# An attention stage and its first value products: order by priorities replaced by an order computed in the kernel from step durations

## The chip, the cores and the metric

The kernel runs on one core of one Trainium2 chip. The metric is the device time of one execution in microseconds (us), shown as the median of the runs. TensorE (PE, with its weight loads as PEld), VectorE (DVE), ScalarE (ACT) and GpSimd (POOL) compute; nearly all transfers are issued from the queue of SyncE (SP).

## What is computed

Everything is float32. Attention comes first, then two gated feed-forward layers on its result:

```python
B, H, S, D = (4, 8, 576, 64)
scores = where(causal, -1e9, q @ k.T / sqrt(D)); a = softmax(scores)
local  = a @ v
q_p    = where(q > 0, q, exp(q) - 1) + 1
mem    = (q_p @ M_prev) / (q_p . z_prev + 1e-6)
x      = sigmoid(beta) * mem + (1 - sigmoid(beta)) * local     # 2304 tokens x 512
x      = (sigmoid(x @ w_gate) * (x @ w_val)) @ w_out           # layer 1, 1536 wide
out    = (silu(x @ w_gate2) * (x @ w_val2)) @ w_out2           # layer 2
```

In most products both operands are held as a high part and a low part, and a product is the sum of three matmuls (high by high, high by low, low by high: `PASSES`). "Value products" are x @ w_val of layer 1; gate products are x @ w_gate.

## The kernel before, in words

**Attention.** The 8 heads of a batch make 4 pairs, two heads side by side on the partitions. A batch is worked in two kinds of units: 2 "head" units, each with the first 256 tokens of two pairs, and 4 "rest" units, each with the last 320 tokens of one pair (in the code, `Unit`, kinds `head` and `rest`; with `SPLIT = 4` all four batches are cut so). There are 24 units. A unit loads its q, k and v (`load`, line 143); turns q and k onto the partitions with TensorE and splits them into high and low parts (`turn`, lines 245 to 259; `turn_tail`, lines 261 to 275, for the last 64 tokens); makes the feature map e of q and scales it by its norm (`prep_e`, `prep_w`, lines 197 to 222), turning it in `turn_e` (lines 224 to 243); makes the scores of a block of 128 tokens and their softmax (`scores`, lines 285 to 338: products at 302 and 316, the running minimum on DVE at 303 and 319, the exponential on ACT at 325 and 330, two small DVE operations on the sums at 333 and 334, the scaling at 338 on POOL or DVE); turns the weights of the softmax (`probs`, lines 340 to 376, products at 355, 363, 370, 374); and sums the memory product and the values (`values`, lines 378 to 406, products at 387 and 396), from where the result goes to the DRAM buffer `xs` (line 408). Copies out of PSUM pass the helper `copy` (line 31 is its ACT branch, 35 and 37 its DVE and free ones), so they have those lines in the trace. PSUM has 8 banks: 3 for scores (`sc`), 3 for turned blocks (`tp`), 1 for `av`, 1 for the value products (`gv`).

The matmuls of line 316 use one half of TensorE's rows each (64 rows, two heads at once); those of line 396 one half of its columns; all others the whole array, but for the 64-token tails.

**Other work in the same stretch.** 24 weight blocks of layer 1 (12 of w_val, 12 of w_gate, each 128 x 512) come as 64-bit numbers and are turned to float32 on ACT and DVE (`Weights.turn`, lines 493 to 511: ACT at 500, four DVE operations at 503, 504, 507 and 511), and stored to the DRAM buffer `ws` (line 562); the w_val blocks are also split into high and low (line 603). The value products of the first 1152 tokens, in four pieces of 256, 320, 256 and 320 tokens, are made as soon as their tokens lie in `xs` (`Moe.load`, line 708; `Moe.values`, line 738, products at 749), each piece in 12 groups of 12 matmuls, each group emptied by ACT into `vo` and stored to the DRAM buffer `vs` (line 758).

**What sets the order.** `Attention.emit` (line 410) gives each step of each unit a due time from the tables `WHEN`, `WHEN0` and `SPAN` (in units of one unit's length) and writes the program in that order; the weight blocks and the four pieces join with due times from `EXTRA` (`Moe.extras`, line 760), the pieces 1 to 3 at 100 or later, and the w_gate loads are held back behind the loads of given units (`Weights.keep`, `gate_weight`). A scheduler of the framework then takes this program order as priorities and sets the real order on every engine, filling gaps with later work by its own estimate of durations. Which engine does a copy or a split is fixed in `ENGINE`, but for a few marked `any`.

**After it**, `Moe.run` (line 1043) makes the last 384 tokens' value products, prepares operands, and runs the two layers (lines 844, 995, 998); its order is pinned by `pinned` (line 953), which chains all instructions of each engine in program order.

Of the kernel before, what the change touches and what calls it, by code (L numbers as in the profile page):

```python
# [1 line left out]
WHEN = {'qk': -2.918, 'zm': -2.8, 'v': -0.622, 'pe': -1.766, 'pw': -1.489, 'pm': -1.092, 't0': -0.87, 't1': -0.45, 'te': 0.857, 's3': 0.004, 's2': 0.265, 's4': 0.5, 's1': 0.704, 's0': 0.85, 'p3': 0.476, 'p2': 0.809, 'p4': 0.938, 'p1': 0.919, 'p0': 1.1, 'v0': 1.112, 'v1': 1.339, 'store': 1.26, ('rest', 'v0'): 1.425, ('rest', 's4'): 0.378, ('head', 'v'): -1.263, ('rest', 'p1'): 0.628, ('rest', 's1'): -0.002, ('head', 'v0'): 1.122, ('rest', 'store'): 2.346, ('head', 's2'): 0.45, ('rest', 's0'): 0.08, ('head', 's4'): 0.733, ('rest', 'v1'): 1.114, ('rest', 'zm'): -2.421, ('rest', 'te'): 0.827, ('rest', 'pw'): -1.506}  # L2
WHEN0 = {'pm': -1.252, 'pe': -1.0, 'pw': -0.99, 'zm': -2.0, 't0': -1.2, 's0': 0.834, 'te': 0.682}
SPAN = {'head': (0.8, 0.85), 'rest': (0.734, 0.75), 'full': (0.866, 1.0)}
MZ = 1
BUFS = {'a_sm': 5, 'a_s': 6, 'a_xo': 1, 'a_pht': 1, 'a_ps': 3, 'a_pst': 3, 'w_raw': 2, 'w_cv': 2, 'm_vo': 2, 'm_gv': 1, 'm_x': 1, 'b_h': 4, 'b_hl': 3}
REUSE = dict(reuse_waits="tile")
SPLIT = 4
LATE = 4
EXTRA = {'gate': 0, 'rate': 0.3, 'w': 7.88, 'dw': 0.128, 'x0': 14.25, 'v0': 7.89, 'x1': 15.52}  # L10
# [32 lines left out]

NOSYNC = mybir.DependencyInfo(mybir.DependencyClass.NoSync, mybir.DependencyReason.DATA)


class Attention:
# [3 lines left out]
    def __init__(self, ctx, banks, tc, q, k, v, M_prev, z_prev, beta, xs):  # L51
# [48 lines left out]
        for r in range(2):  # L100
            t = cst.tile([128, 2, 128], F32R, name=f"qd{r}")
            nc.gpsimd.memset(t.bitcast(F32), 0.0)
            self.qd.append(t)
        g = self.g = cst.tile([128, H], F32, name="g")
# [28 lines left out]
        for p in range(0, self.NP, self.HP):  # L133
            if p < SPLIT * self.HP:
                self.units += [Unit("head", (p + i, p + i + 1)) for i in range(0, self.HP, 2)]
            self.units += [Unit("rest" if p < SPLIT * self.HP else "full", (p + i,)) for i in range(self.HP)]
        for n, u in enumerate(self.units):
            u.n = n
            u.lo, u.hi = dict(head=(0, 4), rest=(2, self.C), full=(0, self.C))[u.kind]
            u.b, u.hp = divmod(u.pairs[0], self.HP)  # L140
        self.st, self.loaded = {}, {}

    def load(self, u, names):
        nc = self.nc
        F, T = self.FULL, self.TAIL
        for n in names:
# [14 lines left out]
            if u.kind == "head":  # L161
# [7 lines left out]
                for c in range(2):  # L169
                    last = nc.sync.dma_start(  # L170
                        out=t[:, 2 * c:2 * c + 2].rearrange("p g h d -> p (g h) d"),
                        in_=src[2 * u.hp:2 * u.hp + 4, 128 * c:128 * c + 128].rearrange("h p d -> p h d"))
            else:
# [6 lines left out]
                last = nc.sync.dma_start(out=t[0:T, F], in_=s[:, 128 * F:].rearrange("h p d -> p h d"))  # L180
            setattr(u, n, t)
            if n == "q":
                self.loaded[u.n] = last.ins

    def prep_m(self, u):
        if u.kind == "rest":
            return
        for p in u.pairs:
            st = self.st.setdefault(p, {})
            mh = st["mh"] = self.mm.tile([128, 128], F32R, tag="mh", name="mh")  # L190
            ml = st["ml"] = self.mm.tile([128, 128], F32R, tag="ml", name="ml")
            m = u.m[:, p % self.HP]
            self.copy("mh", mh, m)
            self.two("ml", u).tensor_sub(ml, m, mh.bitcast(F32))

    def prep_e(self, u):

        nc = self.nc
        c = slice(u.lo, u.hi)
        q = u.q[:, c]  # L200
        u.e = self.ph.tile([128, self.C, 2, self.D], F32, tag="e", name="e")
        e = u.e[:, c]
        nc.vector.tensor_scalar(e, q, 0.0, None, op0=ALU.min)
        nc.scalar.activation(out=e, in_=e, func=ACTF.Exp)
        nc.vector.scalar_tensor_tensor(out=e, in0=q, scalar=0.0, in1=e, op0=ALU.max, op1=ALU.add)

    def prep_w(self, u):
        nc = self.nc
        n, g = u.hi - u.lo, len(u.pairs)
# [3 lines left out]
        e = by(u.e[:, u.lo:u.hi])  # L213
        w = by(self.ph.tile([128, self.C, 2, self.D], F32, tag="w", name="w")[:, 0:n])
        self.two("w", u).tensor_mul(w, e, u.z[:, hs].unsqueeze(1).to_broadcast(shp))
        f = self.sm.tile([128, 2 * self.C], F32, tag="f", name="f")[:, 0:2 * n]
        f = f.rearrange("p (c h) -> p c h", h=2 * g)
        nc.vector.tensor_reduce(out=f, in_=w, axis=mybir.AxisListType.X, op=ALU.add)
        nc.vector.tensor_scalar(f, f, 1e-6, None, op0=ALU.add)
        nc.vector.reciprocal(f, f)  # L220
        nc.vector.tensor_mul(f, f, self.g[:, hs].unsqueeze(1).to_broadcast(shp[:3]))
        nc.vector.tensor_mul(e, e, f.unsqueeze(3).to_broadcast(shp))

    def turn_e(self, u):
        nc = self.nc
        F, T, e = self.FULL, self.TAIL, u.e
        pt = u.pt = self.pht.tile([128, 2, self.S], F32R, tag="pt", name="pt")

        parts = dict(
            head=[[(2 * c + g, 256 * g + 128 * c) for g in range(2) for c in range(2)]],  # L230
            rest=[[(c, 128 * c) for c in range(2, F + 1)]],
            full=[[(c, 128 * c) for c in range(F)], [(F, 128 * F)]],
        )[u.kind]
        for part in parts:
            bank = self.pst.tile([128, 512], F32, tag="tp", name="tp")
            q0, n = part[0][1], 0
            for c, at in part:
                rows = T if c == F else 128
                n += rows
                nc.tensor.transpose(bank[:, at - q0:at - q0 + rows], e[0:rows, c].rearrange("p h d -> p (h d)"),  # L240
                                    self.idf[0:rows, 0:rows])
            self.copy("e", pt[:, 0, q0:q0 + n], bank[:, 0:n])
            nc.vector.tensor_sub(pt[:, 1, q0:q0 + n], bank[:, 0:n], pt[:, 0, q0:q0 + n].bitcast(F32))

    def turn(self, u, g):
# [3 lines left out]
        hp = u.pairs[g] % self.HP  # L249
        bank = self.pst.tile([128, 512], F32, tag="tp", name="tp")  # L250
        for i, t in enumerate((u.q, u.k)):
            for j, c in enumerate(cs):
                at = 128 * (n * i + j)
                self.nc.tensor.transpose(bank[:, at:at + 128], t[:, c].rearrange("p h d -> p (h d)"), self.idf)  # L254
        src = bank[:, 0:256 * n].rearrange("p (k t) -> p k t", k=2)
        to = slice(128 * c0, 128 * (c0 + n))
        hi, lo = (self.qka[:, hp, i, :, to] for i in range(2))
        self.copy("th", hi, src)
# [26 lines left out]
    def scores(self, u, g, i):  # L285
# [41 lines left out]
        else:  # L327
# [4 lines left out]
            r = sm  # L332
# [1006 lines left out]
```

## Time and profile before

| | us |
|---|---|
| median of three runs | 1140.15 (1139.62 to 1140.35) |
| the profiled execution, its time | 1140.23 |
| its span from first to last instruction | 1138.4 |
| attention stage, to the last store of attention | 0 to 362.5 |
| last value products and first operands | 362.5 to 394.5 |
| the two layers | 394.5 to 1138.4 |

The profiled execution is 0.08 us above the median; 1.83 us of its time lie outside the span. In the profile a busy PE is not a PE at its peak: ends of matmuls are modelled and overlap the next ones. In the chain of waits, matmuls that follow each other without a wait are spaced as they were really issued, so a piece of the chain gives the cost of a run of matmuls.

### The profile page before, as it was taken

Reading aid. Unit: us, or ns where it says so; the run is one execution under the profiler, and the core shown is the slowest. Engines: PE = TensorE matmul, PEld = TensorE weight load, DVE = VectorE, ACT = ScalarE, POOL = GpSimd, SP = SyncE. Lnnn points to the kernel's source line nnn. Section 1 sums busy time; section 2 is a strip of 40 time slices with the busy share of each in tenths; the row PEclk is TensorE's granted clock in tenths of the full one; section 3 lists DMA queues with packets and bytes.
Section 4 is the critical chain, followed back from the end, with each engine's and each line's share of the span. In section 5 each row is a group of like instructions: output and inputs, shape, how many; then the busy total and the mean of one; then the engine's idle time right before and its main releaser. Section 6 shows DMA issues by size and latency. Waiting matters only on the chain.

```text
span 1138.4 us, 19089 instructions
## 1 busy us (share of the span) xinstructions
PE 1097.5 (96%) x6416; PEld 995.3 (87%) x6416; DVE 806.4 (71%) x2020; ACT 599.7 (53%) x1472; POOL 167.8 (15%) x209
## 2 busy tenths in 40 slices
PE   7888999899999999999999999999999999999998
PEld 5666877777877899999999999999999999988886
DVE  7799867877966887887765654687877877653332
ACT  5657676566676765555543434555445445332222
POOL 3486543434233000000000000000000000000000
PEclk9689999999999999999999999999999999999999
DMA  5466436535722657666774333334443443654443
GB/s 132 143 180 198 137 90 191 155 119 152 216 57 72 230 153 262 221 218 221 241 256 135 94 95 105 120 94 139 139 149 120 157 132 117 214 172 124 124 124 105
DMA packets 162355, 173.77 MB, mean 153 GB/s; under 512 B 69328, under 2 KB 127696, under 8 KB 162256
## 3 DMA queue, kind: packets, MB, share of 16 engines
q1 hardware_dynamic: 162112, 172.54, 49.4%
q8 instruction: 51, 0.84, 0.3%
q14 instruction: 48, 0.39, 0.1%
q10 hardware_dynamic: 144, 0.00, 0.0%
HBM read 112.20 MB, written 60.29 MB: 152 GB/s over the span
## 4 chain that ended last, share of the span: by engine, by line
PE 77%; DMA 5%; DVE 4%; ACT 3%; issue 1%; SPq 1%; POOLq 0%; POOL 0%; ACTq 0%; DVEq 0%
PE ps L844 37%; PE ps L995 13%; PE ps L998 11%; PE gv L749 5%; PE sc L316 3%; PE av L396 3%; DMA raw<-in_moe_w_gate_dram 2%; PE tp L363 1%; DMA xraw<-xs 1%; PE av L387 1%; PE sc L302 1%; DMA raw<-ws 1%; PE tp L355 1%; PE tp L254 1%; PE tp L240 1%
## 5 line engine op out<-in xcount | busy, mean ns | idle before, releaser
L844 PE MATMUL ps<-xop,wset 128*128 128x384 f32 x2520 | 443.1, 336 | 6.6 <-ACT c L892 6.6
L844 PEld LDWEIGHTS ps<-xop,wset 128*128 128x128 f32 x2520 | 439.8, 188 | 8.9 <-ACT c L892 8.8
L981 DVE TENSOR_TENSOR hl<-hd,hl 128x384 fp32r<-128x384 f32 x144 | 80.3, 558 | 144.3 <-ACT hl L980 143.4
L980 ACT CAST hl<-hd 128x384 fp32r<-128x384 f32 x144 | 74.0, 514 | 179.8 <-PE ps L995 89.4
L892 ACT COPY c<-ps 128x384 f32<-128x384 f32 x180 | 86.2, 479 | 117.0 <-PE ps L844 115.7
L895 DVE TENSOR_TENSOR c<-ps,c 128x384 f32<-128x384 f32 x180 | 99.6, 554 | 43.3 <-ACT c L892 22.1
L749 PE MATMUL gv<-x,w 128*128 128x256 f32 (+2 forms) x720 | 127.1, 322 | 0.3
L749 PEld LDWEIGHTS gv<-x,w 128*128 128x128 f32 x720 | 109.8, 198 | 8.4 <-issue 4.2
L998 PE MATMUL ps<-hl,xop 128*128 128x384 f32 x648 | 114.0, 336 | 0.0
L998 PEld LDWEIGHTS ps<-hl,xop 128*128 128x128 f32 x648 | 112.6, 188 | 0.0
L995 PE MATMUL ps<-xop,hl 128*128 128x512 f32 x486 | 111.2, 389 | 0.0
L995 PEld LDWEIGHTS ps<-xop,hl 128*128 128x128 f32 x486 | 91.2, 188 | 19.0
L338 POOL TENSOR_SCALAR s<-s,sum,omg 128x512 f32<-128x512 f32 (+2 forms) x92 | 76.3, 840 | 105.0 <-DVE sum L334 50.7
L855 ACT ACTIVATE h<-c 128x384 f32<-128x384 f32 x108 | 56.7, 525 | 56.4 <-DVE c L895 53.0
L330 ACT ACTIVATE s<-s,nm 128x256 f32<-128x256 f32 (+3 forms) x128 | 71.8, 563 | 18.6 <-DVE nm L319 18.0
L316 PE MATMUL sc<-qka 64*128 64x128 f32 (+3 forms) x384 | 73.1, 372 | 8.3 <-DVE nm L319 7.4
L319 DVE CUSTOM_DVE_ANT_0 s<-sc,mask 128x256 f32<-128x256 f32 (+3 forms) x128 | 59.6, 484 | 14.8 <-PE tp L355 8.2
L316 PEld LDWEIGHTS sc<-qka 64*128 64x128 f32 x384 | 48.2, 201 | 24.1 <-DVE nm L319 9.2
L500 ACT ACTIVATE a<-raw 128x512 f32<-128x512 f32 x72 | 48.4, 672 | 31.9 <-DMA raw<-in_moe_w_gate_dram 19.2
L31 ACT COPY p<-tp 128x512 f32<-128x512 f32 x96 | 45.3, 496 | 18.1 <-PE av L396 7.7
L507 DVE SCALAR_TENSOR_TENSOR a<-raw,a 128x512 int32<-128x512 int32 x72 | 51.5, 715 | 0.2
L511 DVE SCALAR_TENSOR_TENSOR a<-raw,a 128x512 int32<-128x512 int32 x72 | 51.3, 712 | 0.3
(152 smaller groups left out, 1476.3 us busy)
## 6 DMA issues: line engine op xcount, KB each, us to landing
hs<-h SPq DMA_DIRECT2D x72, 384.0 KB, 4.4
hd<-hs SPq DMA_DIRECT2D x144, 192.0 KB, 2.5
raw<-in_moe_w_val_dram SPq DMA_DIRECT2D x24, 512.0 KB, 4.4
raw<-in_moe_w_gate_dram SPq DMA_DIRECT2D x24, 512.0 KB, 4.3
raw<-in_moe_w_out_dram SPq DMA_DIRECT2D x24, 512.0 KB, 4.3
ws<-a SPq DMA_DIRECT2D x44, 256.0 KB, 2.4
vi<-vs SPq DMA_DIRECT2D x24, 384.0 KB, 5.0
raw<-ws SPq DMA_DIRECT2D x24, 256.0 KB, 5.2
```

Source lines behind the costliest of these rows:

```text
L316: nc.tensor.matmul(o, lhsT=qk[hr, x, 0, qs], rhs=qk[hr, y, 1, 0:n], start=k == 0, stop=k == 2)
L319: nc.vector.tensor_tensor_reduce(out=dsts[h], in0=o, in1=self.mask[:, m0:m0 + n], scale=-scale, scalar=3.0e38, op0=ALU.add, op1=ALU.min, a ...
L330: nc.scalar.activation(out=s, in_=s, func=ACTF.Exp, bias=nm[:, h:h + 1], scale=-1.0, accum_out=sm[:, h:h + 1])
L338: self.two(f"n{i}", u).tensor_scalar(s, s, r[:, h:h + 1], w, op0=ALU.mult, op1=ALU.mult)
L749: nc.tensor.matmul(o, lhsT=w[:, i, k, :], rhs=x[:, j, k, :], start=n == 0, stop=n == 3 * self.KD - 1)
L844: self.nc.tensor.matmul(o, lhsT=w[:, a, i, k], rhs=x[:, b, j, k], start=first and n == 0, stop=n == 5, skip_group_check=True)
L892: nc.scalar.copy(r.c[n], r.banks[0])
L895: nc.vector.tensor_add(r.c[n], r.banks[bank], r.c[n])
L980: nc.scalar.copy(hl[:, 0], h)
L981: nc.vector.tensor_sub(hl[:, 1], h, hl[:, 0].bitcast(F32))
L995: nc.tensor.matmul(y, lhsT=h[:, i, 128 * c:128 * c + 128], rhs=w[:, j].rearrange("p k f -> p (k f)"), **st)
L998: nc.tensor.matmul(y[:, 0:T], lhsT=w[:, i, c, :], rhs=h[:, j, :], **st)
```

## The change

The due times and the framework's scheduling of the attention stage are replaced by a plan that the kernel computes while it is built. Every instruction group (loading one tile, one product group, one copy out of PSUM, one DVE operation, one store) is a `Step` with the engines that may run it and a duration in ns for each; the value products of a group are four steps of 3 matmuls instead of one of 12. `Plan.order` is a list scheduler: it goes forward in planned time, and on each engine takes, among the steps that could start first (within `NEAR` ns), the one with the smallest due time. It keeps count of the buffers, adds a latency per engine from the end of a step to its readers (`LAG`), a cost for changing TensorE between whole array, half rows and half columns (`ENTER`, `LEAVE`), treats a span of POOL and DVE's marked operations as exclusive (`port`), and lets a second engine take a step only at a handicap (`HOLD`). All of it is then issued inside `pinned`, so the order is fixed on PE, DVE, ACT, POOL and SP.

```diff
-SPAN = {'head': (0.8, 0.85), 'rest': (0.734, 0.75), 'full': (0.866, 1.0)}
+SPAN = {'head': 0.975, 'rest': 0.75}
+HOLD = {'dve': 800, 'act': 0, 'pool': 500}
+NEAR = {'pe': 2, 'dve': 1, 'act': 1, 'pool': 1, 'sp': 1}
+SLOW = 0.022
+FREE = dict(pe=4000.0, dve=5100.0, act=4900.0, pool=5200.0, sp=700.0)
-BUFS = {'a_sm': 5, 'a_s': 6, 'a_xo': 1, 'a_pht': 1, 'a_ps': 3, 'a_pst': 3, 'w_raw': 2, 'w_cv': 2, 'm_vo': 2, 'm_gv': 1, ...}
+BUFS = {'a_sm': 5, 'a_s': 6, 'a_xo': 1, 'a_pht': 1, 'a_ps': 3, 'a_pst': 2, 'w_raw': 2, 'w_cv': 2, 'm_vo': 2, 'm_gv': 2, ...}
...
+def away(n, *on):
+    cost = dict(act=0.83 * n + 95, dve=fast(n))
+    return {e: cost[e] for e in on or ("act",)}
+def out(n):
+    return dict(act=0.83 * n + 42, dve=plain(n))
+def either_of(n):
+    return dict(pool=2.06 * n + 165, dve=plain(n))
...
+class Plan:
+    LAG = dict(pe=320.0, dve=125.0, act=150.0, pool=110.0, sp=2300.0)
+    ENTER = dict(h=210.0, c=150.0)
+    LEAVE = dict(h=100.0, c=95.0, t=-80.0)
...
+                        if e != next(iter(s.on)):
+                            t += HOLD[e]
+                        t = max(t, free[e])
+                        if e == "pool" or e == "dve" and s.port:
+                            t = max(t, port)
...
+                    t, n = min(((t, n) for t, n in found if t <= first + NEAR[e]),
+                               key=lambda x: (steps[x[1]].at + (SLOW if e == "pe" and steps[x[1]].mode != mode else 0.0), x[1]))
...
-        nc.vector.tensor_scalar(f, f, 1e-6, None, op0=ALU.add)
-        nc.vector.reciprocal(f, f)
+        add("f2", b, dict(dve=100.0), lambda e: nc.vector.reciprocal(u.f, u.f), [], [R])
...
-        nc.vector.tensor_scalar(r, r, 1e-9, None, op0=ALU.add)
+        add(f"s{i}-sum", at, dict(dve=72.0), lambda e: nc.vector.tensor_reduce(
+            out=st["sum", i][:, 0:r], in_=self.total[:, p, i, 0:r], axis=mybir.AxisListType.X, op=ALU.add), [], keys)
...
+            add(f"s{i}-norm", at, self.normal(cols), lambda e, h=h: normal(e, h), [(SM, h)],
+                [(x, 0)] + ([(x, 1)] if tail else []), port=True)
...
-        for _, _, u, n, g in sorted(order, key=lambda o: o[:2]):
...
+        plan = self.plan_all(moe)
+        with moe.pinned():
+            for step, e in plan.order():
+                step.do(e)
...
-    def keep(self, m, s, after):
-        a = self.number()
-        return a, self.turn(self.fetch(*self.source(0, m, s), after), a) + [lambda: self.store(s, m, a)]
...
+            for k in range(self.KD):
+                plan.add("gv", at, dict(pe=3 * (T / 2.4 + 13.3)), lambda e, f=part, k=k: f(e, k),
+                         [("wv", m, i) for i in range(2)] + [(X, i, k // 2 * 2) for i in range(2)], [(G,)],
+                         [("gv", G)] if not k else [], lag=None if k == self.KD - 1 else -1e3)
+            plan.add("gv-out", WHEN["go"], out(T), empty, [(G,)], [(V,)], [("vo", V)])
+            plan.add("vs", WHEN["go"], dict(sp=360.0), store, [(V,)], [("vs", m, n)])
```

`self.normal(n)` is `dict(pool=0.9 * n + 290, dve=fast(n))`, with `fast(n) = n / 1.92 + 67` and `plain(n) = n / 0.96 + 67`. So every scaling of the softmax may go to POOL first and to DVE second, the block of 128 tokens of the head units included, which `ENGINE` had on DVE (`('head', 'n0'): 'dve'`); and every copy out of PSUM to ACT first and DVE second, the high part of the turned e of the head units included, which `ENGINE` had on DVE (`'e': 'dve'`). The small constants 1e-6 and 1e-9 are no longer added by an operation of their own: they lie in a column that the sum takes in. The due time of a w_gate block is 10 to 21.5 and of a w_val block 5.9 to 7.3, on a scale on which the 24 units take 19.8; the value products have 100 and later; the hold of w_gate loads behind given units is gone. One PSUM bank moves from the turned blocks (3 to 2) to the value products (1 to 2). The rest of the kernel is the same.

## Rows read from the trace of the kernel before

**Rows 1.** The page, busy time of each engine; TensorE's granted clock in 40 slices.

```profile
PE 1097.5 (96%) x6416; PEld 995.3 (87%) x6416; DVE 806.4 (71%) x2020; ACT 599.7 (53%) x1472; POOL 167.8 (15%) x209
...
PEclk9689999999999999999999999999999999999999
```

**Rows 2.** Busy time of each engine by stretch (stretch, length, engines, clock, DMA share, GB/s).

```profile
8.00:114.40 106.40, 92.14 (x554) 69.50 (x553) 94.89 (x284) 67.25 (x184) 62.11 (x65) 0.86 0.58 164
114.40:201.80 87.40, 87.36 (x619) 70.47 (x620) 65.04 (x216) 57.80 (x163) 41.31 (x52) 1.00 0.51 142
201.80:292.60 90.80, 84.30 (x599) 67.48 (x598) 70.28 (x230) 58.17 (x165) 34.81 (x44) 0.96 0.52 148
292.60:362.50 69.90, 67.02 (x470) 50.58 (x469) 53.51 (x191) 47.96 (x141) 25.28 (x31) 1.00 0.31 92
362.50:394.50 32.00, 29.19 (x167) 28.55 (x165) 26.36 (x60) 22.29 (x52) 0.00 (x0) 1.00 0.67 217
394.50:1138.40 743.90, 735.32 (x4008) 707.30 (x4008) 494.32 (x1038) 343.76 (x767) 0.00 (x0) 1.00 0.49 156
```

**Rows 3.** The same stretches, the value products of line 749 alone.

```profile
8.00:114.40 106.40, 19.82 (x104) 16.67 (x104) 0.86 0.58 164
114.40:201.80 87.40, 34.60 (x197) 28.15 (x197) 1.00 0.51 142
201.80:292.60 90.80, 31.72 (x187) 26.83 (x188) 0.96 0.52 148
292.60:362.50 69.90, 16.18 (x95) 13.75 (x94) 1.00 0.31 92
```

**Rows 4.** Chain of waits, 160 to 176 us: shares by line; start, us, what.

```profile
by line: PE gv L749 30.0%; PE sc L316 18.5%; PE av L396 14.7%; PE tp L363 14.6%; PE sc L302 10.3%; PE av L387 2.8%; PE tp L370 2.7%; PE tp L254 2.7%; PE tp L240 2.6%; PE tp L266 1.3%; PE tp L374 0.7%
...
159.96 0.44 PE gv L749 x3
...
164.38 1.77 PE gv L749 x12
...
167.03 2.35 PE av L396 x20
...
169.38 1.02 PE tp L363 x8
...
175.65 0.46 PE sc L302 x2
```

**Rows 5.** Chain of waits, 203 to 216 us.

```profile
204.10 1.43 PE gv L749 x12
...
210.23 0.80 PE av L396 x8
```

**Rows 6.** Groups by line and shape, 0 to 362.5 us (busy us, mean ns; idle before).

```profile
L219 DVE TENSOR_SCALAR f<-f 128x6 f32<-128x6 f32 x16 | 5.4, 337 | 0.1
...
L219 DVE TENSOR_SCALAR f<-f 128x8 f32<-128x8 f32 x8 | 1.5, 188 | 0.0
...
L338 DVE TENSOR_SCALAR s<-s,sum,omg 128x128 f32<-128x128 f32 x32 | 11.6, 398 | 0.2
...
L35 DVE CAST pt<-tp 128x512 fp32r<-128x512 f32 x8 | 5.5, 686 | 0.1
...
L333 DVE TENSOR_SCALAR sum<-sum 128x2 f32<-128x2 f32 x64 | 15.1, 236 | 4.3 <-ACT s L330 4.1
...
L333 DVE TENSOR_SCALAR sum<-sum 128x1 f32<-128x1 f32 x16 | 2.3, 147 | 1.6 <-ACT s L325 1.4
...
L338 POOL TENSOR_SCALAR s<-s,sum,omg 128x512 f32<-128x512 f32 x32 | 28.2, 891 | 63.3 <-DVE sum L334 33.3 <-ACT s L330 11.0 <-DVE sum L333 7.0
...
L338 POOL TENSOR_SCALAR s<-s,sum,omg 128x256 f32<-128x256 f32 x28 | 21.8, 786 | 34.0 <-DVE sum L334 14.0 <-PE sc L316 7.1 <-DVE qd L272 4.9
...
L31 ACT COPY p<-tp 128x512 f32<-128x512 f32 x64 | 36.2, 586 | 15.9 <-PE av L396 7.7 <-PE tp L363 3.9 <-PE tp L355 2.4
```

**Rows 7.** Waits of the SP queue, 0 to 362 us (total us, times, longest).

```profile
SPq L758 <- ACT vo L31: 38.3, 18, 3.9
```

More of the change, by code (lines that the diff above doesn't have):

```diff
@@ L186, in prep_m, with map_steps @@
+    def map_steps(self, u):
         if u.kind == "rest":
             return
[L188 to L205, printed above, removed]
@@ L220, in prep_w @@
-        nc.vector.reciprocal(f, f)
[L221 to L236, printed above, removed]
+        q, E, W, R = ("q", u.n % 2), (f"e{u.n}",), (f"w{u.n}",), (f"f{u.n}",)
@@ new lines, in turned, with run @@
+    def turned(self, name, at, count, do, ev, tile, reads, keys, takes, size, engines, rows=128, writes=()):
+        bank = {}
+        def run(e):
+            bank[0] = self.pst.tile([128, 512], F32, tag="tp", name="tp")
+            do(bank[0])
+        P = f"tp{self.count()}"
+        self.plan.add(name, at, dict(pe=109.0 * count), run, reads, [(P,)] + list(writes), [("tp", P)] + takes, mode="t")
+        for n, (ons, what, r, w) in enumerate(ev):
+            self.plan.add(name + "-out", at, ons, lambda e, what=what: what(e, bank[0]), [(P,)] + r, w)
@@ new lines, in count, with turn_e_steps, do @@
+    def count(self):
+        self.n += 1
+        return self.n
+    def turn_e_steps(self, u):
+        F, T = self.FULL, self.TAIL
+        tile, E = f"pt{u.n}", (f"e{u.n}",)
+        part = [(2 * c + g, 256 * g + 128 * c) for g in range(2) for c in range(2)] if u.kind == "head" else \
+            [(c, 128 * c) for c in range(2, F + 1)]
+        q0 = part[0][1]
+        n = sum(T if c == F else 128 for c, _ in part)
+        def do(bank):
+            u.pt = self.pht.tile([128, 2, self.S], F32R, tag="pt", name="pt")
@@ L294, in scores @@
         if tail:
[L296 to L297 removed]
             half = S // 2
[L299 to L302 removed]
+            read += [(x, b, h) for x in ("dh", "dl") for h in range(2)] + [("dt", b)]
@@ L303, in scores, with one, least @@
+            def one(e, n):
+                if not n:
+                    begin()
+                a = half * n
+                o[n] = self.ps.tile([128, 512], F32, tag="sc", name="sc")[:, 0:half]
+                for k, (x, y) in enumerate(PASSES):
+                    nc.tensor.matmul(o[n], lhsT=u.qd[:, x], rhs=qk[:, y, 1, a:a + half], start=k == 0, stop=k == 2)
+            def least(e, n):
+                a, nm = half * n, st["nm", i]
                 nc.vector.tensor_tensor_reduce(
-                    out=s_t[:, a:a + half], in0=o, in1=self.tmask if a else self.mask[:, 0:half],
```

750 lines of the change are left out of this document (521 added, 229 removed).

## The prediction

> **What bounds the kernel now.** I read the page first: TensorE is busy for 96% of the span, and its granted clock falls below full only in the first tenth [rows 1]. Then I cut the span where a batch of attention ends with its last store; in each stretch the reader should compare the length with the busy time of every engine [rows 2]. The two layers (743.9 us, TensorE busy for 735.32) and the 32.0 us ahead of them are not touched by the change. What can move is the attention stage: four batches of 106.4, 87.4, 90.8 and 69.9 us, 354.5 together.
>
> There TensorE looks busy too, so I ask how much work that is. The chain of waits gives spacings: twelve value products of 320 columns take 1.77 us (147.5 ns each) and of 256 columns 1.43 us, twenty value matmuls of a rest unit 2.35, eight of a head pair 0.80, eight transposes 1.02 [rows 4, 5]. With 147.5 = 320 / 2.4 + 14 I estimate other widths as columns / 2.4 + 14 ns (2.4 GHz is the full clock). The counts come from the code. Full transposes: 24 in each of 8 head units and 24 in each of 16 rest units, 576 x 0.1275 = 73.4 us; 64 half ones at half, 4.1. Scores in half rows, three slots each, two heads side by side, 16 blocks each of 512, 384, 256 and 128 columns: 16 x 3 x (227 + 174 + 121 + 67) ns = 28.3. Tail scores: 96 of 288 columns, 12.9. Memory products: 48 of 256 and 48 of 320 columns, 12.8. Values: 16 x (2.35 + 0.80) = 50.4. Attention is 181.9 us, 45.5 per batch; the four pieces of value products are 288 x 147.5 + 288 x 119 ns = 76.8. TensorE's work is therefore 258.7 of the 354.5 us, 73%.
>
> By batch, the value products counted in each stretch [rows 3] at 76.8 / 583 = 0.132 us give 13.7, 25.9, 24.6 and 12.5 us; the records double a few at the cuts. So the batches hold 59.2, 71.4, 70.1 and 58.0 us of TensorE work: 56%, 82%, 77% and 83% of their lengths. The first is the poor one, and there DVE is busy for 94.89 of 106.4 us, 89%; in the others DVE stands at 74% to 77% [rows 2]. So the first batch is bound by DVE, with POOL at 58%, and the other three mostly by TensorE with gaps between its pieces. The densest piece that I found is 160 to 176 us: its chain never leaves TensorE, and the 25 pieces from 159.96 to 176.1 us, priced as above, are 13.8 us of work in 16.1, 86% [rows 4]. The other 14% are mostly changes between whole array, half rows and half columns, which no order removes entirely.
>
> **The change, part by part.**
>
> Work removed from DVE. The addition to f goes: 5.4 + 1.5 us [rows 6]. The scaling of the head units' small block, 32 on DVE, 11.6 us, goes to POOL as first choice. Eight casts of the turned e, 5.5 us, go to ACT. Together 24.0 us, 6.0 per batch. The first unit's splits on DVE are under 4 us and I leave them out. The sum that takes the place of the second small addition stays on DVE at about the same count (64 + 16), so I take zero for it; it reads twice the columns, and its ends are a gain of 64 x (236 - 147) ns = 5.7 us, if it no longer meets POOL, and as much loss [rows 6].
>
> Work added elsewhere. On POOL 512 columns take 891 ns and 256 take 786 [rows 6]; 128 extrapolate to 733, times 32 is 23.5 us, 5.9 per batch, on an engine that is busy for 62.11, 41.31, 34.81 and 25.28 us [rows 2]: it lies beside other work. ACT gets 8 casts near 0.586 us [rows 6], 4.7 us over the stage, at 63% to 69% busy: nothing on the path.
>
> One row speaks against crediting all of this. The small addition on the sums takes 236 ns with two columns and 147 with one [rows 6]: DVE loses time to something that a second column cannot explain, and the two-column one is where POOL is mostly scaling the neighbouring block. The Trainium skill, "SBUF — State Buffer", section "SBUF: two separate sides", says that DVE and GpSimd share one pair of ports as an exclusive lock for a whole instruction, the loser standing still. By that rule the blocks moved to POOL would lock DVE out about as long as DVE worked on them, and the sum below would be smaller by the first batch's share of 11.6 us, some 3 us; the trace agrees with a loss, not with its size. I credit the whole 24.0, because many of DVE's operations read PSUM and the plan keeps the marked ones apart from POOL.
>
> First batch. DVE's 94.89 us become 88.9. At the same share, 89%, the batch takes 99.7 us: 6.7 gained. The weight blocks are not cheaper, and the w_gate blocks, no longer held back, may come into this stretch; I take zero for that since their due times are later, and up to a tenth of DVE's work there, 9 us, as the bad end. The clock of 0.86 in this batch [rows 2] I leave as it is; a mean of 0.86 between half and full clock is 28% of the batch, 30 us, at 1.2 GHz; at 2.4 GHz those would take 15 us less, and that is an upper end, because DVE bounds there.
>
> Batches two to four. They hold 199.5 us of TensorE work in 248.1, 80%. What keeps them from 86% is order: a group of 12 value products cannot start until ACT has emptied the one bank, and gaps in attention are shorter than a group. Two banks, groups cut into four, and durations near the measured ones attack just that. I take the densest piece's 86% for all three: 199.5 / 0.86 = 232.0, 16.1 gained. The ends are 80% (nothing gained) and 90% (221.7, 26.4 gained); DVE's 188.8 - 18 = 171 us would then be 77% of the time, which the first batch shows to be possible.
>
> Turned blocks with two banks instead of three. There are 8 x 7 + 16 x 9 = 200 groups. A group of four holds its bank for 0.51 us of transposes and at least 0.586 us of ACT [rows 4, 6]. 200 x 1.1 us over two banks are 110 of the stage's 354.5 us, so I take zero; one bank less can gain nothing by itself, and the bad end is the rival below.
>
> SP's queue. All loads and stores stay on it, in the same number, in a fixed order now. Stores of value products wait there for 38.3 us in total today, longest 3.9 [rows 7], and whatever load is behind them waits too. A load is due nearly three units ahead, so I take zero; bad end 3.9 us once in each batch, 16 us.
>
> Tail. After the last store the 32.0 us remain, since their chain starts at that store.
>
> Sum, against the profiled execution: 1140.2 - 6.7 - 16.1 = 1117.4; the w_gate blocks leave the last two batches for earlier gaps, for which nothing is added. I predict **1117 us**; the profiled execution stands 0.08 us above the median, so nothing is corrected.
>
> **The rivals.**
>
> *Dense everywhere.* The plan packs the first batch as well: 258.7 / 0.86 = 301 us instead of 354.5, 53.7 gained, 1086.5 us. For it: TensorE's work is only 73% of the stage, and value products can fill gaps from the first batch on [rows 3]. Against it: DVE would have to do about 260 us in 301 (86%), as dense as in today's first batch, and the plan's POOL times (0.9 x 512 + 290 = 751 ns) are below the measured 891 [rows 6]. Chance 0.22.
>
> *Two banks stall TensorE (slower).* In a fixed order a transpose whose bank is not yet empty holds every matmul behind it. The price is 200 groups times the mean wait: 0.11 us each would undo the forecast gain of 22.8, and 0.2 us gives 40, so 1157 us. It decides as soon as ACT is late by more than 0.11 us against the plan at a typical group. For it: copies take 586 ns against the plan's 467 (0.83 x 512 + 42) [rows 6], 0.12 us late each time one is on the path. Against it: the plan sees the banks and puts value products between, and ACT is a third idle. Chance 0.18.
>
> *No change.* The order on the engines comes out no better than the one of today, or the losses on SP take the gain: 1140 us, within 0.2%, which is about what a measurement of this kernel can tell from no change. For it: the order of today also fills gaps with value products, and has them in all four batches [rows 3]. That would also be the result if the change did not do what it says, and the order stayed near today's. Chance 0.06.
>
> **How the numbers follow.** The forecast (about 1117, own range 1098 to 1133) has 0.54, dense 0.22, no change 0.06, slower 0.18. The range of 8 in 10 reaches past the dense case, to 1082, and up to just past no change, 1145; the rest of the slower case is left out. Forecast and dense are faster by over 0.2%: 0.76; no change 0.06; slower 0.18.
>
> **What would show it.** In the changed kernel the last store of attention near 340 us; the first batch shorter by some 7 us with DVE still near 89%; gv groups broken into threes in the chain; TensorE's share of real work in the later batches near 86%; no L219 on DVE. Transposes waiting for ACT's copies in the list of waits, more than 20 us in all, would show the two banks; value products left over after the last store, or loads of q and k at the head of the chain, would make the prediction wrong.

## The result, and the profile after

| | before | after |
|---|---|---|
| median of 4 runs each, same chip | 1140.25 us (1139.62 to 1144.98) | 1102.74 us (1101.95 to 1108.59) |
| ratio | | 0.9673, interval 0.9631 to 0.9716 |
| profiled execution, its span | 1140.23, 1138.4 | 1101.95, 1099.7 |
| mean granted clock | 0.984 | 0.994 |

Faster by 37.5 us; 1117 was forecast. First the page of the kernel after, against [rows 1].

```profile
PE 1068.5 (97%) x6416; PEld 974.3 (89%) x6416; DVE 789.8 (72%) x1999; ACT 607.7 (55%) x1498; POOL 134.2 (12%) x182
...
PEclk9999999999999999999999999999999999999999
```

TensorE's granted clock no longer falls to 0.6 in the second slice, and POOL, which was to get 23.5 us more, has 33.6 us less. Next the stretches of after, cut like [rows 2] at the last store of each batch, then at the first layer product (columns: stretch, length, PE, PEld, DVE, ACT, POOL, clock, DMA share, GB/s).

```profile
8.00:88.97 80.97, 71.72 (x487) 51.72 (x486) 70.62 (x238) 61.10 (x177) 37.98 (x49) 0.96 0.56 148
88.97:173.68 84.71, 82.56 (x634) 67.29 (x632) 75.49 (x245) 66.25 (x183) 39.88 (x45) 1.00 0.68 196
173.68:244.66 70.98, 69.90 (x552) 55.15 (x552) 62.98 (x216) 55.52 (x159) 28.57 (x36) 1.00 0.61 173
244.66:316.79 72.13, 70.39 (x536) 55.87 (x535) 55.79 (x196) 52.45 (x149) 22.52 (x30) 1.00 0.41 121
316.79:354.51 37.72, 34.38 (x202) 33.74 (x201) 28.11 (x64) 26.17 (x61) 0.00 (x0) 1.00 0.61 197
354.51:1099.70 745.19, 737.10 (x4008) 708.73 (x4008) 494.62 (x1038) 343.36 (x767) 0.00 (x0) 1.00 0.49 156
```

The value products (now line 1158) in the first four stretches and the 5 us behind them, against [rows 3]:

```profile
8.00:88.97 80.97, 7.63 (x36) 6.07 (x36) 0.96 0.56 148
88.97:173.68 84.71, 36.43 (x222) 30.86 (x222) 1.00 0.68 196
173.68:244.66 70.98, 23.22 (x138) 18.80 (x138) 1.00 0.61 173
244.66:316.79 72.13, 25.81 (x148) 21.30 (x149) 1.00 0.41 121
316.79:321.80 5.01, 4.93 (x34) 4.67 (x32) 1.00 0.74 210
```

Stretch by stretch against [rows 2]: first batch 106.4 to 80.97 us, 25.4 less; batches two to four 248.1 to 227.8, 20.3 less; tail 32.0 to 37.7, 5.7 more, of which 5.0 are the 34 value products left over; layers 743.9 to 745.2, 1.3 more; outside the span 0.4 more. The sum is 38.3 less, the difference of the two profiled executions. So the gain lies in attention, and part of the value products is pushed out of it.

Groups by line and shape in attention of after, against [rows 6] (busy us, mean ns; idle before):

```profile
L630 POOL TENSOR_SCALAR s<-s,sum,omg 128x512 f32<-128x512 f32 x25 | 19.3, 782 | 41.8 <-DVE sum L638 19.3 <-ACT s L624 7.6 <-ACT a L846 5.3
...
L630 POOL TENSOR_SCALAR s<-s,sum,omg 128x128 f32<-128x128 f32 x29 | 16.1, 563 | 24.1 <-DVE sum L638 10.9 <-ACT s L624 6.3 <-PE av L729 4.5
...
L630 POOL TENSOR_SCALAR s<-s,sum,omg 128x256 f32<-128x256 f32 x25 | 15.1, 611 | 19.0 <-DVE sum L638 9.3 <-DVE nm L611 4.8 <-ACT s L624 3.0
...
L636 DVE TENSOR_REDUCE sum<-total 128x2 f32<-128x4 f32 x64 | 9.7, 151 | 5.1 <-ACT s L624 4.7
...
L630 DVE TENSOR_SCALAR s<-s,sum,omgt 128x576 f32<-128x576 f32 x11 | 6.6, 601 | 0.0
```

A scaling of 512 columns takes POOL 782 ns where it took 891, one of 384 740 where it took 837 and one of 256 611 where it took 786, but the five of 576 columns left on POOL take 1073 where it was 917; the sum with two columns out of four takes DVE 151 ns where the addition of two took 236. DVE has taken over wide scalings (eleven of 576 columns are shown) while POOL has 29 of the small ones.

**The clock.** In the kernel before, four stretches of 10 us inside the first batch (columns as above) show where it went down:

```profile
30.00:40.00 10.00, 6.98 (x42) 5.19 (x41) 8.63 (x32) 5.22 (x15) 5.67 (x6) 0.82 0.63 182
40.00:50.00 10.00, 9.85 (x35) 6.87 (x33) 5.81 (x21) 5.83 (x16) 7.10 (x7) 0.50 0.51 161
...
60.00:70.00 10.00, 5.89 (x31) 4.46 (x30) 8.79 (x21) 6.25 (x16) 9.45 (x10) 0.86 0.67 199
70.00:80.00 10.00, 10.00 (x66) 8.51 (x65) 9.15 (x27) 6.79 (x17) 8.14 (x7) 0.80 0.45 136
```

The clock fell inside the first of these stretches, in which TensorE was busy for 7.0 of 10 us, and the whole next one has 0.50: 1.2 in place of 2.4 GHz. TensorE then looks 98% busy, with 35 matmuls in 10 us against 77 in the same stretch of after:

```profile
40.00:50.00 10.00, 9.72 (x77) 6.74 (x73) 9.71 (x36) 9.35 (x26) 5.88 (x8) 1.00 0.44 136
```

Over the span (1 - 0.984) x 2 x 1138.4 = 36.4 us passed at 1.2 GHz before and (1 - 0.994) x 2 x 1099.7 = 13.2 us after; in the first batch 29.8 and 6.5.

### The profile page after: what moved, and what is told of

Same layout as the page of the kernel before. It is cut to its first block, busy times and chain, and to the rows that moved or that the text cites. A ratio compares the mean times of both kernels' runs of the same rounds, so it can differ in the third digit from the quotient of the medians.

```text
span 1099.7 us, 19092 instructions
## 1 busy us (share of the span) xinstructions
PE 1068.5 (97%) x6416; PEld 974.3 (89%) x6416; DVE 789.8 (72%) x1999; ACT 607.7 (55%) x1498; POOL 134.2 (12%) x182
## 4 chain that ended last, share of the span: by engine, by line
PE 81%; DVE 8%; DMA 5%; ACT 3%; issue 2%; POOL 1%; SPq 0%; DVEq 0%; ACTq 0%; POOLq 0%
PE ps L1259 38%; PE ps L1410 13%; PE ps L1413 12%; PE gv L1158 5%; PE av L729 3%; PE sc L607 3%; PE tp L680 2%; DMA xraw<-xs 1%; PE tp L510 1%; PE tp L668 1%; DMA xr<-xs 1%; DVE s L611 1%; PE sc L580 1%; PE av L721 1%; DMA hd<-hs 1%
## 5 line engine op out<-in xcount | busy, mean ns | idle before, releaser
L1158 PE MATMUL gv<-x,w 128*128 128x256 f32 (+1 forms) x576 | 98.0, 310 | 0.3 <-ACT vo L73 0.3
L624 ACT ACTIVATE s<-s,nm 128x256 f32<-128x256 f32 (+4 forms) x144 | 84.1, 586 | 13.4 <-DVE nm L611 12.0
L1158 PEld LDWEIGHTS gv<-x,w 128*128 128x128 f32 x576 | 81.7, 192 | 5.1 <-issue 3.2
L630 POOL TENSOR_SCALAR s<-s,sum,omg 128x128 f32<-128x128 f32 (+3 forms) x102 | 67.2, 668 | 90.2 <-DVE sum L638 40.9
L752 ACT COPY p<-tp 128x512 f32<-128x512 f32 (+3 forms) x119 | 56.7, 495 | 11.3 <-PE tp L680 6.7
L607 PE MATMUL sc<-qka 64*128 64x128 f32 (+3 forms) x384 | 51.8, 367 | 2.7 <-DVE nm L611 2.4
L857 DVE SCALAR_TENSOR_TENSOR a<-raw,a 128x512 int32<-128x512 int32 x72 | 50.5, 701 | 0.3
L853 DVE SCALAR_TENSOR_TENSOR a<-raw,a 128x512 int32<-128x512 int32 x72 | 50.0, 694 | 0.1
L607 PEld LDWEIGHTS sc<-qka 64*128 64x128 f32 x384 | 32.0, 199 | 15.9 <-issue 9.7
```

The costliest lines, as they stand in the source:

```text
L607: nc.tensor.matmul(o[h], lhsT=qk[hr, x, 0, qs], rhs=qk[hr, y, 1, 0:n], start=k == 0, stop=k == 2)
L624: nc.scalar.activation(out=s, in_=s, func=ACTF.Exp, bias=st["nm", i][:, h:h + 1], scale=-1.0, accum_out=self.total[:, p, i, h, 0:1])
L630: self.on(e).tensor_scalar(s, s, st["sum", i][:, h:h + 1], w, op0=ALU.mult, op1=ALU.mult)
L1158: nc.tensor.matmul(st["o"], lhsT=w[:, p, k, :], rhs=x[:, q, k, :], start=k == j == 0, stop=k == self.KD - 1 and j == 2)
```

## The experiments

Each of twelve kernels changes one thing in the kernel after or before; e5 changes two, and e10 joins e7 and e9. Times are medians of 4 executions (6 of e2, 10 of b1); the ratio is to the kernel before, run beside it (medians 1137.62, 1136.44 and 1138.92 us in the three groups: e1 to e3 and b1; e4 to e6 and b2; e7 to e10), so ratios compare better than times. What a kernel costs or is worth is below the difference of its median to 1102.74; the kernel after was not run again beside the three groups, and by the ratios, against its 0.9673, the costs come out 0.3 to 4.4 us larger. "Fill" is when the last 384 tokens' value products begin, 321.6 us in the kernel after: attention and all earlier value products are done.

**e1: weight blocks early.** What first sets the length of the first batch?

```diff
-WHEN = {..., 'w': 5.906, ...}
+WHEN = {..., 'w': -1.0, ...}
```

> The changed kernel with the due time of the w_val blocks at -1 instead of 5.9, so that they come ahead of attention. Deferral theory: the first batch got 25 us shorter because 7 of its 12 weight blocks, each about 2.4 us of DVE, moved out of it; put back, the first batch grows from 81 to 95-101 us, the later ones do not get it all back, and the time is 1115-1122 us. Rival (the gain of the first batch is the denser order, whatever the blocks do): first batch within 4 us of 81, time 1101-1106 us.

Measured: 1114.52 us, 0.9809 (0.9769 to 0.9849); fill 334.3. The stretch of its first batch; then ACT's operation that opens a weight block, in the first batch of e1, of after and of before.

```profile
8.00:111.69 103.69, 83.10 (x546) 60.80 (x544) 91.67 (x280) 71.40 (x198) 44.45 (x53) 0.88 0.66 190
```

```profile
8.00:111.69 103.69, 9.50 (x14) 0.88 0.66 190
```

```profile
8.00:88.97 80.97, 3.29 (x5) 0.96 0.56 148
```

```profile
8.00:114.40 106.40, 8.15 (x12) 0.86 0.58 164
```

The first batch is back at 103.7 us with 14 blocks in it, and with DVE at 88% and a clock of 0.88, all near [rows 2], and the batch is 2.7 us longer than the most that was expected: it is the due time of w_val's blocks that shortens the first batch by nearly all of its 25 us. The value products, which need these blocks, move with them: the first batch has 104 records of them before, 102 in e1 and 36 after. But half comes back: the later batches take 78.0, 74.8 and 69.9 us and nothing is left over, so deferring the blocks is worth 11.8 us net.

**b1: the same in the kernel before.** There the rate at which weight blocks come due was changed.

```diff
-EXTRA = {'gate': 0, 'rate': 0.3, ...}
+EXTRA = {'gate': 0, 'rate': 1.0, ...}
```

> The kernel before, with the loads of the w_val blocks held behind later units (rate 1.0 instead of 0.3 units per block), so that they come over some 130 us instead of 90. Deferral theory: the first batch gets shorter by 10-18 us and the time falls to 1122-1132 us, without any plan. Rival (the order on the engines is what counts): 1136-1144 us.

Measured: 1147.18 us, 1.0093 (1.0064 to 1.0122). In the profiled execution, at 1140.27 us the fastest of the ten, the first batch has 9 blocks and ends 8.8 us earlier, but the fourth takes 82.1 us in place of 69.9 and ends where it did (362.6). Under the old scheduler deferring three blocks moves the work and gains nothing; seven, as in the kernel after, were not tried there.

**e2: banks back.**

```diff
-'a_pst': 2, ... 'm_gv': 2
+'a_pst': 3, ... 'm_gv': 1
```

> The changed kernel with the banks of before: three for turned blocks, one for value products; the plan is made anew. Theory that the second bank for value products carries them: with one bank fewer of them fit in the gaps, 30-45 us of them are left behind the last store of attention, attention itself ends up to 10 us earlier, time 1122-1137 us. Rival from the prediction (two banks for turned blocks stall TensorE): the third bank back makes it faster, 1090-1100 us.

Measured: 1126.4 us, 0.991 (0.9876 to 0.9944); fill 346.4. Attention alone ends 18.6 us sooner, at 298.2, but 216 value products are left behind it and not 34; the 182 more, at 0.132 us, are 24 us of work, so attention is no denser with the third bank. The stretch of what is left, and the wait in it:

```profile
299.60:346.40 46.80, 34.61 (x217) 30.24 (x217) 5.41 (x10) 11.76 (x29) 0.00 (x0) 1.00 0.32 105
```

```profile
PEld gv L1158 <- ACT vo L73: 16.3, 18, 1.8
```

With one bank TensorE stands still for 12 of the 46.8 us, since each group waits for ACT to empty the last one. The bank moved from the turned blocks to the value products is worth 23.7 us in this plan.

**b2: the banks of after in the kernel before.**

```diff
-'a_pst': 3, ... 'm_gv': 1
+'a_pst': 2, ... 'm_gv': 2
```

> The kernel before with two banks for turned blocks and two for value products. Theory that the banks only pay together with an order that uses them: 1132-1150 us. Rival (the second bank for value products carries much of the gain by itself): 1112-1125 us.

Measured: 1199.36 us, 1.0536 (1.0493 to 1.0579), with a clock of 0.945: 132 us at 1.2 GHz. Under the old scheduler the same move costs 60 us, more than either branch gave. Matmuls that turn blocks wait there for copies of turned blocks on ACT and DVE for 16.2 us in the list of waits, 3.1 in the kernel before and 5.2 in the kernel after. So the mechanism of the rival "two banks stall TensorE" shows under the old scheduler and not in the planned kernel. Its price does not show: 96 us more at 1.2 GHz than before are worth up to 48 of the 60, and the two were not separated.

**e3: groups of twelve.**

```diff
-            for k in range(self.KD):
-                plan.add("gv", at, dict(pe=3 * (T / 2.4 + 13.3)), lambda e, f=part, k=k: f(e, k), ...)
+            plan.add("gv", at, dict(pe=12 * (T / 2.4 + 13.3)), lambda e, f=part: [f(e, k) for k in range(self.KD)], ...)
```

> The changed kernel with a group of value products as one step of 12 matmuls instead of four of 3. Theory that the small steps matter: 1.4 to 1.8 us of value products then stand ahead of attention's own products each time, attention ends 15-20 us later and the leftover goes, time 1112-1120 us. Rival (TensorE has the same work in any cut): 1100-1105 us.

Measured: 1108.12 us, 0.9759 (0.9707 to 0.9812), which overlaps the interval of after; fill 326.9. Groups cut into four are worth about 5 us, at the limit of what can be told, and between what the two branches gave. The value products are used up at 272 us here, and in the last batch TensorE is busy for 54.5 of 59.5 us.

**e4: the planned order as priorities only.**

```diff
-        with moe.pinned():
-            for step, e in plan.order():
-                step.do(e)
+        for step, e in plan.order():
+            step.do(e)
```

> The changed kernel with its plan written out in the planned order, but without the pinning, so that the framework's scheduler sets the final order on every engine from it, as before. Theory that the order on the engines, not the other edits (banks, small steps, constants), carries the gain: at least half of the 37 us goes, 1120-1140 us. Rival (the banks and the small steps carry it): 1100-1110 us.

Measured: 1162.7 us, 1.0221 (1.0173 to 1.0269): 60 us slower than after, and slower than before, which neither branch gave. Its first two batches:

```profile
8.00:111.23 103.23, 91.97 (x517) 66.89 (x517) 91.43 (x272) 71.10 (x196) 52.62 (x56) 0.85 0.61 170
111.23:230.60 119.37, 115.49 (x795) 94.95 (x795) 80.17 (x255) 68.43 (x189) 32.96 (x41) 0.97 0.61 180
```

The framework's scheduler, given the plan's order, pulls value products forward (all are done by 282 us, attention's values only at 378) and DVE's other work into the first batch. Its timeline has 287 changes of TensorE between whole array, half rows and half columns up to the end of attention; before has 263, after 187. With these banks and steps nothing of the gain is left when the order is not kept on the engines. The bank layout of after by itself costs the old scheduler 60 us (b2) and is in e4 too; the planned order as priorities with the banks of before was not run, so how much of e4's loss is the banks stays open.

**e5: more changes of mode.** The three passes of a block's score products become three steps, and the plan sees no price for a change and prefers one.

```diff
-SLOW = 0.022
+SLOW = -1.0
...
-    ENTER = dict(h=210.0, c=150.0)
-    LEAVE = dict(h=100.0, c=95.0, t=-80.0)
+    ENTER = {}
+    LEAVE = {}
...
-            add(f"s{i}", at, dict(pe=3 * (n / 2.4 + 15)), products, ...)
+            for k in range(3):
+                add(f"s{i}", at, dict(pe=n / 2.4 + 15), lambda e, k=k: products(e, k), ...)
```

> The changed kernel with the score products cut into three steps, the plan's costs for changing TensorE's rows and columns at zero and its preference turned round, so that a plan of the same length by its own durations alternates: 260 visits and returns instead of 187; the kernel before had 263. Theory that changes between whole array and half rows cost 0.2-0.35 us each and that fewer of them are a main part of the gain: 73 more cost 15-25 us, 1117-1128 us. Rival (changes hide among the other waits): 1098-1108 us.

Measured: 1115.46 us, 0.9799 (0.9762 to 0.9837); 274 changes; fill 338.6. TensorE's weight loads of the score products, in after and in e5:

```profile
L607 PEld LDWEIGHTS sc<-qka 64*128 64x128 f32 x384 | 32.0, 199 | 15.9 <-issue 9.7 <-DVE nm L611 3.7 <-DVE qka L514 0.6
```

```profile
L608 PEld LDWEIGHTS sc<-qka 64*128 64x128 f32 x384 | 35.0, 204 | 21.5 <-issue 16.9 <-DVE nm L612 2.2 <-DVE qka L514 0.6
```

87 more changes go with 12.7 us, 0.15 us each; the idle time before these loads that nothing visible explains ("issue") grows from 9.7 to 16.9 us. The split kernel also has 29 us at 1.2 GHz against 13, so 0.15 us is a rough upper bound for the change itself; the 7.2 us of "issue" give 0.08 us. The time lies between the two branches.

**e6: scalings on POOL alone.**

```diff
-        self.normal = lambda n: dict(pool=0.9 * n + 290, dve=fast(n))
+        self.normal = lambda n: dict(pool=0.9 * n + 290)
```

> The changed kernel with every scaling of the softmax on POOL, none on DVE (37 of 144 are on DVE now). Theory that a second engine for them shortens the way from scores to turned blocks: 6-12 us slower, 1108-1115 us. Rival (POOL is not on the path, DVE is, so DVE gets time back): 1095-1102 us.

Measured: 1109.96 us, 0.9747 (0.9702 to 0.9791), overlapping after; fill 329.9. POOL spends 108.9 us on all 144 scalings. The free choice between two engines is worth some 7 us, at the limit of what can be told.

**e7: no price of changes.** Score products stay one step.

```diff
-SLOW = 0.022
+SLOW = 0.0
...
-    ENTER = dict(h=210.0, c=150.0)
-    LEAVE = dict(h=100.0, c=95.0, t=-80.0)
+    ENTER = {}
+    LEAVE = {}
```

> The plan is computed as if a change of TensorE between whole array, half rows and half columns cost nothing (ENTER and LEAVE empty, SLOW 0); score products stay one step of three passes. If the fewer changes (187 against 263) come from the prices in the plan, more changes return and at 0.15 to 0.2 us each the time rises with them: 40 more would give about 1110. If they come from the score products being one step, issued in an order that is then kept, the number stays within 10 of 187 and the time within 6 us of 1102.7.

Measured: 1109.95 us, 0.9745 (0.9722 to 0.9768); fill 328.6. The timeline has 193 changes, within 10 of 187, yet the time is 7.2 us up, just outside what the second branch gave. So the fall from 263 changes to 187 is not the price's doing. It goes with score products being one step in a kept order: e4, without the kept order, has 287 changes, and e5, with split steps, 274; but e5 also turned the preference round, so the split by itself was not run. What the price does for the rest of the order was not separated from the scatter between plans (see e10).

**e8: value products early.**

```diff
-WHEN = {..., 'gv': 100.0, ...}
+WHEN = {..., 'gv': 10.0, ...}
```

> The four pieces of value products get due time 10 to 13 in place of 100 to 103, so they go ahead of attention from the middle of the stage on, and are used up before its end, as they were in the kernel before to a smaller part (95 records of 583 in its last batch). If they are worth something as the work of last choice that fills gaps to the end, the last batches, left without filling, stretch: batch stores near 89, 174, 275 and 335, last fill ending near 340, time about 1120 to 1125. If only the amount of TensorE work counts, whenever it is done, time within 6 us of 1102.7.

Measured: 1113.95 us, 0.9795 (0.9762 to 0.9828); fill 330.7 (the expectation's 340 stands for this point). The value products are done at 243 us. The stretch from there to the fill, and the chain of waits in it, then the same chain of the kernel after, 245 to 321 us:

```profile
245.00:330.70 85.70, 76.27 (x574) 51.94 (x572) 68.85 (x255) 69.12 (x201) 38.59 (x51) 1.00 0.27 70
...
by line: PE av L729 18.8%; ACT s L624 13.2%; ACT p L752 9.4%; PE tp L680 7.3%; issue 6.2%; PE sc L607 5.0%; PE av L721 4.7%; PE tp L510 3.6%; DMA xr<-xs 3.3%; ACT pt L752 2.6%; ACT qka L752 2.3%; ACT wset L32 1.8%; DVE pt L493 1.7%; POOL s 
```

```profile
by line: PE gv L1158 27.7%; PE av L729 15.5%; PE tp L680 9.9%; PE sc L607 9.8%; DMA xr<-xs 6.7%; DMA xraw<-xs 6.3%; PE sc L580 4.7%; PE av L721 4.0%; PE tp L489 3.4%; PE tp L668 3.3%; PE tp L510 3.3%; PE tp L693 2.7%; issue 1.9%; ACT s L624
```

Without value products the chain runs through values, the exponential and the copies on ACT, at a full clock and with no engine busy for more than 76.27 of 85.7 us. Kept to the end they are the chain's largest piece. The batches end at 89.2, 173.7, 273.3 and 331.3 us, within 4 us of what was expected. Keeping them as work of last choice is worth 9 us of fill and about 11 of time: the first theory, at half the time that it gave.

**e9: weight blocks still later.**

```diff
-WHEN = {..., 'w': 5.906, ...}
+WHEN = {..., 'w': 8.0, ...}
```

> The due time of w_val's weight blocks goes from 5.906 to 8.0 (e1 with the sign turned). If deferring DVE's weight work is what shortens the first batch, and it is exhausted there (five blocks are left in it), the first batch stays at 81 us and the second shortens by up to 8 us, but the value products start later and 10 us of them are left over: time 1100 to 1110. If more deferral keeps paying, under 1099.

Measured: 1103.7 us, 0.9684 (0.9654 to 0.9714), not to be told from after; fill 322.6. Its first batch takes 76.4 us, not the 81 expected, its second 80.2, and its attention ends at 310.05, 6.7 us sooner than after, and then:

```profile
310.05:322.60 12.55, 11.99 (x83) 11.73 (x81) 3.17 (x6) 5.55 (x13) 0.00 (x0) 1.00 0.67 218
```

All but one of these 83 matmuls are value products that are left, and the fill begins 1 us later than in after. Where the value products take every free place on TensorE, a shorter attention only leaves more of them behind.

**e10: e7 and e9 in one.**

> e7 and e9 in one: due time 8.0 and no price for changes, the shortest attention of the plans tried beside the kernel after. If the two edits add up, time is the sum of their differences to 1102.7; as an improvement it would have to come under 1099 to be told from the kernel after.

Measured: 1117.09 us, 0.981 (0.9785 to 0.9834); fill 339.3. The sum of the two differences would have been 1110.9, so the edits do not add. Two stretches of its second batch:

```profile
90.00:100.00 10.00, 5.14 (x23) 3.15 (x22) 7.51 (x24) 3.33 (x10) 1.25 (x2) 0.60 0.71 183
100.00:110.00 10.00, 5.96 (x30) 4.18 (x31) 7.26 (x18) 5.49 (x15) 4.08 (x4) 0.50 0.43 128
```

TensorE is half idle there, and its clock is at 1.2 GHz for nearly all of 20 us. But this place does not explain the cost: the second batch takes 88.8 us, 4.1 more than in after, and that of e7 takes 91.1. The rest is in the third batch (76.8 us, 5.8 more), the fourth (75.5, 3.4 more) and 58 value products left behind it, and why the edits do not add stays open. So of the small differences between plans (e3, e6, e7) only the sign is likely, and no run beat the kernel after.

## Why the prediction was right, and where its sum was not

The forecast held: faster, within the range, 14 us above the measured time. But the gain of the profiled executions is 38.3 us where 22.8 was summed, and its largest piece, in the first batch, came by a term put at zero. That the total still lies near 1117 owes something to luck: losses put at zero as well, in the tail, the layers and outside the span, took 7.4 us back. The kernel that the sum describes is rather e1, where the weight blocks stay early: 1114.52 us, with 2.7 us gained in the first batch and 25.5 in the other three. By its steps:

- **What bounds the kernel.** Right. Layers, time outside the span and the tail without its leftover moved by 2.4 us in all.
- **First batch, 6.7 us forecast, 25.4 measured: the term that failed.** The model was sound: DVE's share was to stay at 89%, and it is 70.62 of 80.97, 87%. Its load was wrong: 88.9 forecast, 70.62 measured. "The weight blocks are not cheaper ... I take zero for that since their due times are later" looked only at w_gate blocks that might come in, not at w_val blocks that might go out: 12 blocks became 5 (the rows of e1). DVE's four operations on them fell from 33.2 us (6.95, 7.49, 9.44 and 9.27 on lines 503, 504, 507 and 511) to 10.5 (1.65, 3.05, 3.11 and 2.73 on lines 849, 850, 853 and 857): 22.6 of the fall of 24.3. What the prediction did count, 6.0 us of other DVE work, hardly shows there: 1.7 us are left for it, and in e1, with the blocks early, the batch gains 2.7 us and not 6.7. The clock, held back as an upper end of 15 us, came with the load: 23.3 us fewer at 1.2 GHz are worth at most half of that. DVE's load accounts for the fall without it, since its share of the batch is about the same at either clock: 91.4 of 103.2 us at 0.85 in e4, and in e7 71.6 of 81.0 at 1.00, no shorter than after at 0.96. Net of what returns later, the step is worth 11.8 us.

```profile
8.00:89.03 81.03, 69.54 (x496) 49.88 (x494) 71.63 (x249) 59.65 (x178) 36.19 (x48) 1.00 0.52 133
```

- **Batches two to four, 16.1 forecast, 20.3 measured.** Right in mechanism. At the prediction's own prices the value products of the three (222, 138 and 148 by 0.132 us) and 45.5 us of attention each make 203.6 us of work in 227.8, 89%, where 86% was taken and 90% was the end. In e1 it is 199.1 us in 222.6, 89% as well, so this does not hang on the deferred blocks. That "no order removes entirely" the mode changes stands, but three in ten of them went (263 to 187). DVE did not fall to 171 us there: with the deferred blocks it has 194.3 (188.8 before), and 89% of the second and third batch.
- **DVE's 24 us less, POOL's 23.5 more.** DVE: the four batches sum to 264.9 us against 283.7 [rows 2], 18.8 less, near the 24.0, but in part by luck. The additions to f (6.9 us) and the casts of e (5.5) went as forecast. The scalings on DVE did not fall by 11.6 us; they rose from 13.7 to 20.3, since 29 of the 32 small ones went to POOL but DVE has 34 wide ones where it had 4. The four operations on weight blocks got shorter, 63.7 to 58.2 us over all 24, which was not forecast. POOL went the other way from the forecast: its scalings are 108 before and 107 after, but fell from 91.0 to 72.8 us, and some of the splits of x and of M_prev went to other engines. The doubt behind the 236 and 147 ns of [rows 6] was well placed: the two-column addition takes 388 ns in the 21 of 64 cases in which a POOL operation runs beside it and 161 in the others. The sum in its place takes 151, 5.4 us less in all, the size of the good end given there, but not by its condition. It still meets POOL in 24 of 64 cases and takes 151 in these as in the rest; the plan does not mark it as one to be kept apart; and in e4, where no order is kept, it takes 150. So it is the other operation (TENSOR_REDUCE for TENSOR_SCALAR) that gains, not the plan. The Trainium skill, "SBUF — State Buffer", section "SBUF: two separate sides", says that the two engines lock each other out of a shared pair of ports for a whole instruction, on DVE's side only for some kinds of operation; the trace agrees in that the addition lost time beside POOL and the sum does not. In e4, with the same steps, POOL's scaling of 512 columns takes 928 ns against 782 in the kept order; for 128 columns it is the other way, 492 against 563.

```profile
L636 DVE TENSOR_REDUCE sum<-total 128x2 f32<-128x4 f32 x64 | 9.5, 150 | 10.6 <-ACT s L624 10.4
L630 POOL TENSOR_SCALAR s<-s,sum,omg 128x512 f32<-128x512 f32 x25 | 23.0, 928 | 68.1 <-DVE sum L638 25.4 <-DVE f L456 10.9 <-ACT qka L752 10.4
```

- **Turned blocks with two banks, zero taken, rival at 1157.** Zero for the turned blocks fits: with three of them attention is no denser (e2), and transposes wait for ACT's copies for 4.3 us in the list of waits, where more than 20 would have shown the rival. The longest of these waits:

```profile
PE tp L668 <- ACT p L752: 2.3, 2, 1.6
```

  The bank moved to the value products is worth 23.7 us; the prediction had it inside its 16.1.
- **SP's queue, zero taken.** The stores' wait is of the same size as in [rows 7], with a second one beside it; one load of q, 2.9 us at the start of the first batch, is on the chain, and no load of k.

```profile
SPq L1168 <- ACT vo L73: 35.3, 22, 5.1
SPq L1168 <- ACT p L752: 16.1, 5, 7.2
```

- **Tail, zero taken, 5.7 us measured.** The prediction named value products left over as a sign that it would be wrong; 34 were. e9 shows that such a leftover keeps TensorE at work, 11.99 of 12.55 us.
- **The rivals.** "Dense everywhere" (1086.5) lies 16 us below the measured time and the forecast 14 above it. Its place was right, not its reason: the first batch did shorten, because DVE's load left it, hardly because TensorE got denser; its work there is 45.5 + 36 x 0.132 = 50.3 us in 80.97, 62% against 56%. "No change" was to come if the plan did not set the order; e4 is that case, and it is slower than before, with the banks in it.

What the runs show: without the kept order nothing is gained with these banks (e4); deferred weights are worth 12 us, the bank 24, value products kept for last 11. The 87 changes of e5 cost 13 at most; what the 76 fewer of the change are worth was not run. These are losses from single steps back and do not add to 37.5, since each makes another plan.

## What to carry to other kernels

Before crediting an engine's busy share in a stretch, list which of its work is due there and which may be moved, out as well as in: the cheapest gain is work that need not be done in the bound stretch. Keep independent matmuls as filling until the end, and check that what is left over keeps TensorE at work. Order, banks and due times belong together: a bank layout that wins 24 us in a kept order cost 60 us under another scheduler. Before crediting a shorter operation to the order, look at whether it is still the same operation.

## What the runs showed of the hardware

The clock moved more than the prediction, which left it as it was, had it: before has 36.4 us at 1.2 GHz and after 13.2. In before it fell inside the stretch from 30 to 40 us, with TensorE busy for 6.98 of 10 us, and the stretch behind stood at 0.50; in e10 it fell at 92 us, with TensorE busy for 7.32 of the 10 us up to there. At 1.2 GHz TensorE can look 98% busy with half the matmuls. b2's 132 us at 1.2 GHz are the most of any run. The price of leaving and entering half rows was not expected as a number: some 0.15 us a change at most, of which 0.08 us shows as unexplained idle before the weight loads. The Trainium skill, "TensorEngine Tiling (Array Packing)", section "Key Properties", says that a change of tiling mode drains TensorE; the idle time in e5 agrees, and gives a size. A two-column TENSOR_SCALAR on DVE took 388 ns beside a POOL operation and 161 without one; a TENSOR_REDUCE of two columns out of four took 151 in both cases, which was not expected either.
